# Turning x, k and q by transfers inside SBUF in a fused sparse-attention and maxout kernel

## The chip, the cores and the metric

One Trainium2 chip, one core of it. The metric is device time in microseconds (us) of one execution of the whole program. The kernel before took 181.66 us, the median of three runs (181.26 to 181.75). Engines are named as in the profile: PE is TensorE (PEld its weight loads), DVE is VectorE, ACT is ScalarE, POOL is GpSimd, SP is SyncE, which issues nearly all transfers; its queue appears as SPq.

## The reference

Inputs q, k, v have 4 batches, 8 heads, 768 positions of width 64. Each position attends to its neighbours less than 16 away and to 24 block summaries (k by maximum, v by mean, over 32 positions). The output goes through a maxout layer.

```
k_sum = k.reshape(B, H, nb, block, D).max(axis=3)        # block = 32, nb = 24
v_sum = v.reshape(B, H, nb, block, D).mean(axis=3)
scores_l = scale * q @ k.T, masked to |i - j| < 16
scores_s = scale * q @ k_sum.T + log(block)
a = softmax(concat(scores_l, scores_s)); attn = a @ concat(v, v_sum)
x = attn with the heads side by side                      # 3072 x 512
out = maximum(x @ w1, x @ w2) @ w_out                     # 512 -> 1024 -> 512
```

## The kernel before

**Stages.** The work of a batch is cut into four pairs of heads (`hp`) and three groups of 256 positions (`grp`). For each batch and pair, `load_kq` and `load_v` (L310, L317) bring k, q and v into SBUF as float32. `prep` (L404) casts k and q to bf16 (tile `kqb`), has PE turn them into a PSUM bank by `transpose` (op "turn", L422 to L431; k as three transposes of float32 pairs, q as six of bf16), and "place" copies them from the bank into `kx` and `qx` (DVE for k, ACT for q after batch 0). DVE then takes the block maxima (L449). `scores` (L470) multiplies on PE, ACT takes the exponential into `pb`, DVE masks it. `values` (L528) multiplies with `vx` on PE; DVE takes the reciprocal and scales into `xs` (L550, L552). After each second pair, PE turns the 128 x 512 block of x into a bank by four transposes (L562), and a copy (DVE after batch 0) brings it to `xt` (L567). `maxout` (L631) runs on `xt`: per batch and group four "hidden" steps (PE, then Relu on ACT) and "out" steps on PE, a copy from the bank and a store. Here maximum(h1, h2) is written as h1 + relu(h2 - h1), the first term through a product w1 x w_out that is made once.

**v.** `vx` holds v at even and at odd 64-position offsets. `cast_v` writes the even half; `spread_v` (L338) makes the odd half from it by three copies ("odd v", L352 to L363: 64 partitions by 3168 elements, 32 by 2640, 32 by 528) and spreads the sums of v. With engine "S" a copy is a transfer on SP (`move`, L386).

**Order.** The order of instructions is not written out by hand. `Plan` (L73) takes every operation with an engine, a cost, a priority and the buffers that it reads and writes, and lists them greedily, earliest possible first, by its own costs; each engine then runs its list strictly in order. Buffers come from rings of fixed size (`Ring`, L30); a DMA waits in SP's list for its source and its free target. Attention of batch b has priority 1000 b and on, `maxout` of batch b 1000 b + 1500 and on, so that maxout of one batch fills PE beside the attention of the next. The string `CFG` (L21) says which engine does what: `lod` is the engine of "odd v" of batches 1, 2, 3, `lk`, `lq` those of the casts.

```
op("PE", J * 0.056, turn, read=[src], write=[ps], prio=prio, label=f"turn {'kq'[n]}{tag}")      # L431
op("PE", 0.23, turn, read=[x], write=[xp], prio=prio, label=f"turn x{tag}")                     # L566
```

Of the kernel before, what the change touches and what calls it, by code (L numbers as in the profile page):

```python
# [13 lines left out]
BF16 = mybir.dt.bfloat16  # L14
# [7 lines left out]
    kc="DAPA", qc="AAAA", kp="DDDD", qp="AAAADAAA", tl="DDDD", od="DDDD", se="AAAA", sr="PPPP", vc="PPPP",  # L22
    wd="PDDD", w1b="PPAD", w1t="DADD", wo="AADD", xt="AADDDD", z="DAAA", kv=0.2, sp=0.7, ones=1, on="DDD", w=(30,
    31, 50, 51, 200, 201), wt=25, g0=(10, 30, 210), g1=(20, 30, 40), w1o=450, mx=1500, woc=600, wdp=30, lk="ADDP",
    lq="AAPA", lod="SSS", lse="DDD", lsr="DDS", lvc="DPPPDDAPPAPA", ltl="DDPD", ld=500,
)
ENG = {"D": "DVE", "A": "ACT", "P": "POOL"}

# [118 lines left out]
def kernel(  # L147
# [14 lines left out]
    nc = tc.nc  # L162
    B, H, S, D = 4, 8, 768, 64
# [10 lines left out]
    op = plan.op  # L174
# [4 lines left out]
    def tiles(name, n, shape, dt):  # L179
        return [const.tile(shape, dt, name=f"{name}{i}") for i in range(n)]  # L180
# [5 lines left out]
    def bank(buf, n=512, dt=F32):  # L186
        a = bank_tile[:, buf.slot]
        return (a if dt is F32 else a.bitcast(BF16))[:, 0:n]

    def spread(a, *dims):  # L190
        return bass.AP(a.tensor, a.offset, [a.ap[0], *dims])
# [5 lines left out]
    kqb = Ring(tiles("kqb", 4, [128, J * 2 * D], BF16))  # L197
    kxr = Ring(tiles("kx", 4, [128, KW], BF16))
    qxr = Ring(tiles("qx", 4, [128, 2, S], BF16))
    pbr = Ring(tiles("pb", 11, [128, 4, 192], BF16))  # L200
    vfr = Ring(tiles("vf", 4, [128, 2, NM, D], F32))
    vxr = Ring(tiles("vx", 2, [128, NT, H, VW], BF16))
    stg = Ring(tiles("sums", 1, [128, H, VW], BF16))
    ksr = Ring(tiles("ks", 2, [128, nb], BF16))
    xsr = Ring(tiles("xs", 4, [128, 2, 2, 2, D], BF16))
    xtr = Ring(tiles("xt", 6, [128, KC, GT], BF16))
    gr = Ring(tiles("g", 3, [128, FC, GT], BF16))
# [184 lines left out]
    def copy(engine, us, aps, label, port=True, **kw):  # L392
        engine = ENG[engine]
        us = us if isinstance(us, float) else us[engine[0]]
        def fn():
            o, i = aps()
            {"DVE": nc.vector.tensor_copy, "ACT": nc.scalar.copy,  # L397
             "POOL": nc.gpsimd.tensor_copy}[engine](out=o, in_=i)
        op(engine, us, fn, label=label, port=port, **kw)
# [4 lines left out]
    def prep(b, hp, prio, k_on, q_on, kp, qp, tail_on):  # L404
        kx[b, hp], qx[b, hp] = Buf(kxr), Buf(qxr)
        tag = f"{b}{hp}"
        pss = []
        for n, eng in enumerate((k_on, q_on)):
            f, src, ps = kqin[b, hp, n], Buf(kqb), Buf(banks, "kq")
            pss.append(ps)  # L410

            def cast(f=f, src=src, n=n):
                if n:
                    return (src.ap[:].rearrange("p (j h d) -> p h j d", h=2, d=D),
                            f.ap[:].rearrange("p h (j d) -> p h j d", d=D))
                return (src.ap[:].rearrange("p (i h d j) -> p h i j d", h=2, d=D, j=2),
                        f.ap[:].rearrange("p h (i j d) -> p h i j d", d=D, j=2))

            copy(eng, {"D": 0.6, "A": 0.85 if n else 1.06, "P": 0.8 if n else 1.05}, cast,
                 read=[f], write=[src], prio=prio, label=f"cast {'kq'[n]}{tag}")  # L420

            def turn(src=src, ps=ps, n=n):  # L422

                a, to, one = src.ap[:], bank(ps, S, BF16), identity
                if n == 0:
                    a, to, one = a.bitcast(F32), bank(ps), ident32
                for j in range(J if n else J // 2):
                    nc.tensor.transpose(out=to[:, 128 * j:128 * j + 128],  # L428
                                        in_=a[:, 128 * j:128 * j + 128], identity=one[:])

            op("PE", J * 0.056, turn, read=[src], write=[ps], prio=prio, label=f"turn {'kq'[n]}{tag}")  # L431

        kps, qps = pss

        def order(ps, *dims):
            return spread(bank(ps, S, BF16), *dims)

        def kt():

            return kx[b, hp].ap  # L440

        def pairs(at, step, n):
            return free(kt(), at, [256, NM], [step, 2], [1, n])

        kmain, ks, kwrap = Buf(Ring([None])), Buf(ksr), Buf(Ring([None]))
        copy(kp, {"D": 0.56, "A": 0.8}, lambda: (
            pairs(128, 192, 64), order(kps, [2, 128], [256, 3], [1, 2])),
           read=[kps], write=[kx[b, hp], kmain], prio=prio, port=False, label=f"place k{tag}")
        op("DVE", 0.95, lambda: nc.vector.tensor_reduce(  # L449
            out=ks.ap[:],  # L450
            in_=free(kt(), 128, [256, NM], [192, 2], [32, 2], [1, 32]),
            axis=AX.X, op=ALU.max),
           read=[kmain], write=[ks], prio=prio, label=f"max k{tag}")
        copy(tail_on, {"D": 0.18, "P": 0.15, "A": 0.25}, lambda: (
            kt()[:, 256 * NM + 128:256 * NM + 160], kt()[:, 128:160]),
           read=[kmain], write=[kx[b, hp], kwrap], prio=prio, label=f"wrap k{tag}")
        copy(tail_on, {"D": 0.27, "P": 0.45, "A": 0.5}, lambda: (
            pairs(192, 64, 32), pairs(320, 64, 32)),
           read=[kmain, kwrap], write=[kx[b, hp]], prio=prio, label=f"tails k{tag}")
        op("DVE", 0.24, port=True, fn=lambda: nc.vector.tensor_copy(  # L460
            out=pairs(224, 64, nb),
            in_=ks.ap[:].rearrange("p (a b n) -> p a b n", a=1, b=1).to_broadcast([128, NM, 2, nb])),
           read=[ks], write=[kx[b, hp]], prio=prio, label=f"sums k{tag}")
        for a in range(2):
            r = slice(64 * a, 64 * a + 64)
            copy(qp[a], {"D": 0.96, "A": 0.8}, lambda a=a, r=r: (
                qx[b, hp].ap[r, a, :], order(qps, [1, 128], [128, J])[r]),
               read=[qps], write=[qx[b, hp]], prio=prio, port=False, label=f"place q{tag}")

# [58 lines left out]
    def values(b, hp, grp, pb, prio, xt_on="D"):  # L528
        ps, tag = Buf(banks, "av"), f"{b}{hp}{grp}"

        def av():
            return bank(ps)[:, 0:4 * (D + 1)].rearrange("p (u a d) -> p u a d", u=2, a=2)

        def mm():
            for u in range(2):
                for a in range(2):
                    for par in range(2):
                        nc.tensor.matmul(out=av()[:, u, a, :],  # L538
                                         lhsT=pb.ap[:, 2 * u + a, 64 * par:64 * par + 128],
                                         rhs=vx[b].ap[:, 4 * grp + 2 * u + par, 2 * hp + a, 0:D + 1],  # L540
                                         start=(par == 0), stop=(par == 1))

        op("PE", 0.24, mm, read=[pb, ready[b, hp]], touch=[vx[b]], write=[ps], prio=prio, label=f"values {tag}")
        inv = Buf(invr)
        if hp % 2 == 0:
            xs[b, grp] = Buf(xsr)
        if hp == 0:
            xt[b, grp] = Buf(xtr)
        x, x_t = xs[b, grp], xt[b, grp]
        op("DVE", 0.18, lambda: nc.vector.reciprocal(out=inv.ap[:], in_=av()[:, :, :, D:D + 1]),  # L550
           read=[ps], write=[inv], prio=prio, label=f"inv {tag}")
        op("DVE", 0.42, lambda: nc.vector.tensor_tensor(  # L552
            out=x.ap[:, hp % 2], in0=av()[:, :, :, 0:D],
            in1=inv.ap[:].to_broadcast([128, 2, 2, D]), op=ALU.mult),
           read=[ps, inv], write=[x], prio=prio, label=f"x {tag}")
        if hp % 2 == 0:
            return
        xp = Buf(banks, "x")

        def turn():  # L560
            for n in range(4):
                nc.tensor.transpose(out=bank(xp, 512, BF16)[:, 128 * n:128 * n + 128],  # L562
                                    in_=x.ap[:, n // 2, n % 2].rearrange("p a d -> p (a d)"),
                                    identity=identity[:])

        op("PE", 0.23, turn, read=[x], write=[xp], prio=prio, label=f"turn x{tag}")  # L566
        copy(xt_on, {"D": 0.42, "A": 0.62}, lambda: (  # L567
            x_t.ap[:, hp - 1:hp + 1, :].rearrange("p h n -> p (h n)"), bank(xp, 512, BF16)), read=[xp], write=[x_t], prio=prio, port=False, label=f"xt {tag}")
# [115 lines left out]
    def attention(b, base):  # L684
        pbs = {}
        for hp in range(NP):
            p = base + 20 * hp
            prep(b, hp, p, CFG["lk"][hp], CFG["lq"][hp], "D", "AA", CFG["ltl"][hp])
            for grp in range(NG):
                pbs[hp, grp] = scores(b, hp, grp, p + 5 + grp, "DVE")  # L690
            for grp in range(NG):
                values(b, hp, grp, pbs[hp, grp], p + 10 + grp)

    def first_attention():
        pbs = {}
# [64 lines left out]
```

## Time and profile before

| what | value |
|---|---|
| median of three runs | 181.66 us (181.26 to 181.75) |
| span of the profiled execution, first to last instruction | 181.2 us |
| difference of the two, what lies around the span | 0.46 us |
| PE busy | 163.5 us, 1658 matmuls |
| ACT, DVE, POOL busy | 117.9, 106.6, 34.8 us |
| granted TensorE clock | 1.000 |
| moved by DMA | 33.96 MB, 187 GB/s over the span |

The profiled execution's own time is its span plus what lies around it; no separate time is given for it, so the span is set against the median. In the profile, "busy" of PE is modelled from pipelined matmuls: a single matmul's listed duration holds its latency, and what it takes from PE in a stream is read from the chain of waits, where pieces follow each other without overlap. The time of a transfer "to landing" runs from its issue to the event that tells that its data is there.

### The profile page before, as it was taken

The page shows a single profiled execution, that of the slowest core. Times are in us where ns is not written, and L with a number is a line of the kernel's source. Part 1 is how long each engine was busy: PE and PEld are TensorE (multiplying, and loading weights), DVE is VectorE, ACT ScalarE, POOL GpSimd, SP SyncE. Part 2 cuts the span into 40 slices and gives each one's busy share as a digit, 9 for nine tenths or more (in the row PEclk, how much of TensorE's full clock was granted, in tenths as well). Part 3 has the DMA queues.
Part 4 walks back from the last instruction along what each step waited for, and adds up shares of the span by engine and source line. Part 5 has one row for each costly group of instructions (what it writes and reads, how often), then busy time and mean ns, then how long its engine had stood idle before and what let it go on. Part 6 is the DMA issues. An engine that isn't in the chain of part 4 may idle for free.

```text
span 181.2 us, 4246 instructions
## 1 busy us (share of the span) xinstructions
PE 163.5 (90%) x1658; PEld 117.7 (65%) x1658; DVE 106.6 (59%) x314; ACT 117.9 (65%) x190; POOL 34.8 (19%) x61
## 2 busy tenths in 40 slices
PE   0496575999899999999999999999999999999992
PEld 0475475999355555688677685686786766575762
DVE  6699995977679775699796760388774400000000
ACT  8786965998739964289896642599975334352521
POOL 7776576010152000241070000001000000000000
PEclk9999999999999999999999999999999999999999
DMA  5999999999999999998996320340200113030203
GB/s 179 301 293 295 375 387 359 234 299 371 237 314 304 187 312 322 339 257 228 300 281 202 88 113 0 121 90 0 90 32 4 58 58 99 21 116 0 116 4 116
DMA packets 42820, 33.96 MB, mean 187 GB/s; under 512 B 26096, under 2 KB 36784, under 8 KB 42800
## 3 DMA queue, kind: packets, MB, share of 16 engines
q1 hardware_dynamic: 42656, 33.63, 64.4%
q8 instruction: 13, 0.21, 0.5%
q10 hardware_dynamic: 144, 0.07, 0.1%
q14 instruction: 7, 0.06, 0.1%
HBM read 25.17 MB, written 6.29 MB: 174 GB/s over the span
## 4 chain that ended last, share of the span: by engine, by line
PE 74%; DMA 13%; ACT 4%; SPq 4%; DVE 3%; issue 1%; ACTq 0%; DVEq 0%
PE banks L667 23%; PE banks L639 17%; PE banks L660 11%; DMA wf<-in_moe_w_dram 6%; DMA wf<-in_moe_w_out_dram 6%; PE banks L538 5%; PE banks L428 5%; PE banks L492 4%; PE banks L623 3%; PE banks L562 2%; PE banks L368 2%; SPq L580 2%; ACT qx L241 2%; DVE ks L449 1%; SPq L608 1%; DVE vx L397 1%
## 5 line engine op out<-in xcount | busy, mean ns | idle before, releaser
L667 PE MATMUL banks<-wo,g 128*128 128x512 bf16 (+2 forms) x208 | 46.8, 362 | 0.0
L639 PE MATMUL banks<-xt,wd 128*128 128x256 bf16 x384 | 46.3, 273 | 0.0
L639 PEld LDWEIGHTS <-wd 128*128 128x128 bf16 x384 | 36.7, 98 | 5.2
L644 ACT ACTIVATE g<-banks 128x512 bf16<-128x512 f32 x48 | 28.3, 597 | 9.9 <-PE banks L639 9.6
L397 ACT COPY o<-banks 128x512 f32<-128x512 f32 (+2 forms) x25 | 14.0, 564 | 29.8 <-PE banks L667 29.6
L504 ACT ACTIVATE pb<-banks 128x512 bf16<-128x512 f32 x48 | 27.3, 600 | 8.7 <-PE banks L492 7.1
L667 PEld LDWEIGHTS <-g 128*128 128x128 bf16 x208 | 18.2, 97 | 15.7
L397 ACT COPY qx<-banks 64x768 bf16<-64x768 bf16 x31 | 24.5, 791 | 1.8 <-PE banks L428 1.2
L660 PE MATMUL banks<-w1o,xt 128*128 128x512 bf16 (+2 forms) x104 | 24.2, 363 | 0.0
L397 ACT CAST kqb<-kqf 128x768 bf16<-128x768 f32 x18 | 16.1, 894 | 6.2 <-DMA kqf<-in_q_dram 3.5
L397 DVE COPY o<-banks 128x128 f32<-128x128 f32 x1 | 0.3, 292 | 32.2 <-PE banks L667 32.2
L552 DVE TENSOR_TENSOR xs<-banks,inv 128x256 bf16<-128x256 f32 x48 | 18.7, 413 | 0.2
L538 PEld LDWEIGHTS <-pb 128*128 128x128 bf16 x384 | 15.7, 97 | 4.7 <-ACT pb L504 1.1
L538 PE MATMUL banks<-vx,pb 128*128 128x65 bf16 x384 | 17.9, 193 | 0.9 <-ACT pb L504 0.9
L492 PE MATMUL banks<-qx,kx 128*128 128x128 bf16 (+2 forms) x208 | 16.8, 217 | 0.1
L492 PEld LDWEIGHTS <-kx 128*128 128x128 bf16 x208 | 14.1, 99 | 4.1 <-DVE kx L397 0.6
L397 DVE COPY xt<-banks 128x512 bf16<-128x512 bf16 x22 | 9.1, 423 | 10.5 <-PE banks L562 10.1
L449 DVE TENSOR_REDUCE ks<-kx 128x24 bf16<-128x768 bf16 x16 | 15.1, 941 | 0.2
L660 PEld LDWEIGHTS <-xt 128*128 128x128 bf16 x104 | 9.7, 98 | 8.0
L428 PE MATMUL banks<-identity,kqb 128*128 128x128 bf16 x96 | 8.3, 225 | 7.2 <-ACT kqb L397 7.2
L397 POOL CAST vx<-vf 128x768 bf16<-128x768 f32 x10 | 8.2, 824 | 32.3 <-DMA vf<-in_v_dram 32.1
L428 PEld LDWEIGHTS <-kqb 128*128 128x128 bf16 x96 | 6.5, 100 | 7.9 <-ACT kqb L397 7.4
(65 smaller groups left out, 179.5 us busy)
## 6 DMA issues: line engine op xcount, KB each, us to landing
kqf<-in_k_dram SPq DMA_DIRECT2D x16, 384.0 KB, 6.5
kqf<-in_q_dram SPq DMA_DIRECT2D x16, 384.0 KB, 5.6
vf<-in_v_dram SPq DMA_DIRECT2D x16, 384.0 KB, 6.5
out_dram<-o SPq DMA_DIRECT2D x19, 256.0 KB, 2.0
wf<-in_moe_w_dram SPq DMA_DIRECT2D x4, 1024.0 KB, 11.1
wf<-in_moe_w_out_dram SPq DMA_DIRECT2D x2, 1024.0 KB, 10.4
vx<-vx SPq DMA_DIRECT2D x3, 396.0 KB, 6.8
out_dram<-o SPq DMA_DIRECT2D x4, 224.0 KB, 3.3
```

The source lines that it names most:

```text
L397: {"DVE": nc.vector.tensor_copy, "ACT": nc.scalar.copy, "POOL": nc.gpsimd.tensor_copy}[engine](out=o, in_=i)
L428: nc.tensor.transpose(out=to[:, 128 * j:128 * j + 128], in_=a[:, 128 * j:128 * j + 128], identity=one[:])
L449: op("DVE", 0.95, lambda: nc.vector.tensor_reduce(out=ks.ap[:], in_=free(kt(), 128, [256, NM], [192, 2], [32, 2], [1, 32]), axis=AX.X, op= ...
L492: nc.tensor.matmul(out=o[:, :, n0:n1], lhsT=w, rhs=qx[b, hp].ap[:, :, c:c + n1 - n0], start=(mask_on != "PE"), stop=(mask_on != "PE" or (i ...
L504: op("ACT", 0.7, lambda: nc.scalar.activation(out=pv(), in_=bank(ps).rearrange("p (i w q) -> p i w q", w=2, q=64), func=ACT.Exp, scale=scale),
L538: nc.tensor.matmul(out=av()[:, u, a, :], lhsT=pb.ap[:, 2 * u + a, 64 * par:64 * par + 128], rhs=vx[b].ap[:, 4 * grp + 2 * u + par, 2 * hp ...
L552: op("DVE", 0.42, lambda: nc.vector.tensor_tensor(out=x.ap[:, hp % 2], in0=av()[:, :, :, 0:D], in1=inv.ap[:].to_broadcast([128, 2, 2, D]), ...
L623: nc.tensor.matmul(out=bank(ps), lhsT=w[:, at:at + 128], rhs=wo[f // 2].ap[:, f % 2, :], start=(f == 0), stop=(f == FC - 1))
L639: nc.tensor.matmul(out=bank(ps)[:, 256 * s:256 * s + 256], lhsT=wd[n].ap[:, c, 128 * s:128 * s + 128], rhs=x.ap[:, c, :], start=(c == 0), ...
L644: op("ACT", 0.6, lambda n=n, ps=ps: nc.scalar.activation(out=g.ap[:, 2 * n:2 * n + 2, :].rearrange("p f n -> p (f n)"), in_=bank(ps), func ...
L660: nc.tensor.matmul(out=bank(ps, c1 - c0), lhsT=x.ap[:, c, sl], rhs=w1o[c].ap[:, cols], start=(c == 0), stop=False)
L667: nc.tensor.matmul(out=bank(ps, c1 - c0), lhsT=g.ap[:, f, sl], rhs=wo[f // 2].ap[:, f % 2, cols], start=False, stop=(f == FC - 1))
```

## The change

x of batches 1 to 3, and k and q of batches 2 and 3, are turned by a transposing DMA from SBUF to SBUF on SP's queue (`dma_start_transpose`) in place of PE transposes into PSUM. For k and q the target is a new ring `kt` of two tiles, from which "place" copies in place of the bank; k is cast without the pairing that the float32 transposes needed. For x the target is `xt` itself, so the copy from the bank goes. "odd v" of batch 1 moves from SP to DVE, of batch 2 from SP to POOL. The ring `pb` goes from 11 to 9 tiles. The planner's costs of the new operations are in the diff.

```diff
-    lq="AAPA", lod="SSS", lse="DDD", lsr="DDS", lvc="DPPPDDAPPAPA", ltl="DDPD", ld=500,
+    lq="AAPA", lod="DPS", lse="DDD", lsr="DDS", lvc="DPPPDDAPPAPA", ltl="DDPD", ld=500,
+    turn="20 21 22 23 30 31 32 33", lx="SSS",
...
-    pbr = Ring(tiles("pb", 11, [128, 4, 192], BF16))
+    pbr = Ring(tiles("pb", 9, [128, 4, 192], BF16))
...
+    ktr = Ring(tiles("kt", 2, [128, J, 128], BF16))
...
+            by_dma = f"{b}{hp}" in CFG["turn"]
+            f, src, ps = kqin[b, hp, n], Buf(kqb), Buf(ktr) if by_dma else Buf(banks, "kq")
...
-                if n:
+                if n or by_dma:
...
-            op("PE", J * 0.056, turn, read=[src], write=[ps], prio=prio, label=f"turn {'kq'[n]}{tag}")
+            if by_dma:
+                op("SP", 1.0, lambda src=src, ps=ps: nc.sync.dma_start_transpose(out=ps.ap[:], in_=src.ap[:]),
+                   read=[src], write=[ps], prio=prio, label=f"turn {'kq'[n]}{tag}")
+            else:
+                op("PE", J * 0.056, turn, read=[src], write=[ps], prio=prio, label=f"turn {'kq'[n]}{tag}")
...
-            return spread(bank(ps, S, BF16), *dims)
+            return spread(ps.ap[:].rearrange("p j t -> p (j t)") if by_dma else bank(ps, S, BF16), *dims)
...
-        copy(kp, {"D": 0.56, "A": 0.8}, lambda: (
-            pairs(128, 192, 64), order(kps, [2, 128], [256, 3], [1, 2])),
+        copy(kp, {"D": 0.88, "A": 0.83, "P": 0.85} if by_dma else {"D": 0.56, "A": 0.8}, lambda: (
+            pairs(128, 192, 64), order(kps, [1, 128], [128, 6]) if by_dma else order(kps, [2, 128], [256, 3], [1, 2])),
...
+        if xt_on == "S":
+            op("SP", 0.7, lambda: nc.sync.dma_start_transpose(
+                out=x_t.ap[:, hp - 1:hp + 1, :].rearrange("p h (u n) -> p (h u) n", u=2),
+                in_=x.ap[:].rearrange("p h u a d -> p (h u a d)")),
+               read=[x], write=[x_t], prio=prio, label=f"xt {tag}")
+            return
...
-                values(b, hp, grp, pbs[hp, grp], p + 10 + grp)
+                values(b, hp, grp, pbs[hp, grp], p + 10 + grp, CFG["lx"][b - 1])
```

More of the change, by code (lines that the diff above doesn't have):

```diff
@@ L408, in prep @@
         for n, eng in enumerate((k_on, q_on)):
-            f, src, ps = kqin[b, hp, n], Buf(kqb), Buf(banks, "kq")
+            by_dma = f"{b}{hp}" in CFG["turn"]
+            f, src, ps = kqin[b, hp, n], Buf(kqb), Buf(ktr) if by_dma else Buf(banks, "kq")
             pss.append(ps)
             def cast(f=f, src=src, n=n):
-                if n:
+                if n or by_dma:
                     return (src.ap[:].rearrange("p (j h d) -> p h j d", h=2, d=D),
@@ L417, in cast @@
                         f.ap[:].rearrange("p h (i j d) -> p h i j d", d=D, j=2))
-            copy(eng, {"D": 0.6, "A": 0.85 if n else 1.06, "P": 0.8 if n else 1.05}, cast,
+            copy(eng, {"D": 0.6, "A": 0.85 if n or by_dma else 1.06, "P": 0.8 if n or by_dma else 1.05}, cast,
                  read=[f], write=[src], prio=prio, label=f"cast {'kq'[n]}{tag}")
@@ L465, in prep @@
             r = slice(64 * a, 64 * a + 64)
-            copy(qp[a], {"D": 0.96, "A": 0.8}, lambda a=a, r=r: (
+            copy(qp[a], {"D": 0.88, "A": 0.83, "P": 0.85} if by_dma else {"D": 0.96, "A": 0.8}, lambda a=a, r=r: (
                 qx[b, hp].ap[r, a, :], order(qps, [1, 128], [128, J])[r]),
```

## The prediction

> **What bounds the kernel now.** I read the page's busy row by slices first, then the table of stretches, then the chain of waits.
>
> ```profile
> PE   0496575999899999999999999999999999999992
> DMA  5999999999999999998996320340200113030203
> ```
>
> A slice is 4.5 us. PE is full from about 36 us to the end; the transfers fill the first 20 slices (to about 92 us) and are light after. The table of stretches puts numbers to it (us of the stretch, then busy us of PE, PEld, DVE, ACT, POOL, the clock, the DMA share, GB/s):
>
> ```profile
> 36.00:60.00 24.00, 23.42 (x192) 16.02 (x191) 18.12 (x39) 18.53 (x30) 5.46 (x8) 1.00 1.05 303
> 60.00:82.00 22.00, 22.00 (x241) 14.47 (x240) 15.89 (x49) 13.75 (x21) 3.41 (x4) 1.00 1.10 282
> 82.00:100.00 18.00, 18.00 (x208) 13.66 (x207) 14.87 (x44) 15.32 (x26) 3.57 (x7) 1.00 0.92 253
> 100.00:120.00 20.00, 20.00 (x191) 13.94 (x188) 10.05 (x32) 10.26 (x17) 0.00 (x0) 1.00 0.29 84
> 120.00:145.00 25.00, 25.00 (x302) 18.68 (x300) 17.09 (x59) 18.34 (x32) 0.72 (x2) 1.00 0.11 38
> ```
>
> PE has no idle time from 60 us on and the clock is full: in these stretches, where all removed work lies, PE sets the pace and its work taken away is time taken away, as long as nothing new makes it wait. Pieces of the chain of waits (start, us on the chain, what) give what an operation takes from PE in a full stream:
>
> ```profile
> 74.47 0.45 PE banks L562 x8
> ...
> 124.25 0.34 PE banks L428 x6
> ...
> 125.90 0.33 PE banks L428 x3
> ```
>
> Eight x transposes take 0.45 us, 56 ns each; the six of one q take 0.34, the three of one k 0.33. The 219 ns that the group table gives for one such matmul hold its latency, so I don't use them.
>
> **What is removed.** From PE: 18 turns of x (batches 1 to 3, three groups, two pairs of heads) of four transposes, 72 x 0.056 = 4.0 us; 8 turns of q (0.34) and 8 of k (0.33), 5.4 us. Together **9.4 us**, all between 74 and 145 us. From DVE 18 copies to `xt` (0.42 each), 7.6 us, no bound of itself. From SP six "odd v" transfers.
>
> **What is added, and what hides it.** DVE takes the three "odd v" of batch 1: its copy of 32 x 3168 elements took 978 ns, so 0.98 + 0.82 + 0.16 = 2.0 us, hidden since PE is the bound there and DVE has 6 us free in 22. POOL takes those of batch 2: 32 x 792 elements took 862 ns, 1.09 ns per element, so 3.4 + 2.9 + 0.6 = 6.9 us. In the order of the new program some 11 us of PE work stand between the last cast of that v and the first "values" of batch 2, and POOL had 3.4 to 3.6 us of work in stretches of 18 to 22 us: hidden, with about 2 us to spare; if late, PE waits for the excess. "place k" reads SBUF with a stride in place of packed pairs: between 0.55 us (now) and 0.93 (the one DVE copy of q, 934 ns), at most 8 x 0.38 = 3.0 us on DVE, which loses 7.6; nothing. "place q" stays near 0.79 on ACT. Casts of k lose their pairing: at most some tenths. `pb` at 9 tiles: three groups ahead in place of nearly four; the program now interleaves "values" of batch 1 earlier, and PE has its other work there; nothing.
>
> **The unknown: the transposing DMA itself.** No row shows one. A turn of k or q moves 192 KB, one of x 128 KB. The nearest rows are the plain SBUF to SBUF moves (the last number is us to landing):
>
> ```profile
> vx<-vx SPq DMA_DIRECT2D x3, 396.0 KB, 6.8
> ...
> vx<-vx SPq DMA_DIRECT2D x3, 165.0 KB, 4.8
> vx<-sums SPq DMA_DIRECT2D x2, 198.0 KB, 3.2
> ```
>
> The last one is the same size and ran at 117 us, beside nothing else: 3.0 to 3.5 us. While loads are in flight, a load takes 5.6 (q) or 6.5 us (k, v). The bounds are 2.0 us (the median of the stores) and 9.6 us (the slowest of the `vx` moves). I take **3.2 us in a quiet queue and 6.0 beside loads**, the row nearest in size and kind.
>
> What that costs: `kt` has two tiles, one for k and one for q of a pair, so the turn of the next q is issued only when both halves of the last are placed. The cycle is landing + 2 x 0.79 us of "place q" + 0.5 us of handover (estimate: a semaphore and half of a running 0.6 us instruction on ACT). PE hides it if the work that its list has between the first scores of one pair and of the next is longer. By the chain's pieces (scores 0.225, values 0.24, a hidden step 0.87, half an out 0.86, sums 1.29) the list of the new program has between successive pairs of batches 2 and 3: 6.6, 13.5, 6.4, then 7.2, 6.4, 6.0, 5.7 us. (The 6.0: 3 scores, 4 values, 3 out, 2 hidden.) Batch 2 is turned while the loads of batch 3 run: 6.0 + 2.1 = 8.1, so PE waits 1.5 + 0 + 1.7 = 3.2 us. Batch 3 has a quiet queue: 3.2 + 2.1 = 5.3, below every period, so 0. The x turns have a whole batch of time before `maxout` reads them and cost PE nothing, but they stand in SP's list between the turns of k and q, each waiting for DVE's "x". While ACT or DVE waits for a turn at its "place", the exp, Relu, masks and scalings behind it wait too, and PE for these; in batch 3 ACT has 20.7 us of work (12 exp, 8 halves of q, 8 Relu, 4 copies) beside 21.8 us of PE work, so I add 0.5.
>
> **Sum**: 181.2 - 9.4 + 3.2 + 0.5 = 175.5 us of span; with the 0.46 around it **176.0 us**. If every turn is hidden it is 171.8 + 0.46 = 172.3, the low end.
>
> The Trainium skill has two pages that disagree on the price. "Advanced Engine Details and Errata", X-Bar Transpose (TRN2), says that such transfers are as fast as plain ones, 350 to 400 GB/s; an estimate from it is 0.5 us of moving for 192 KB, and the sum stays as it is. "VectorE: DVE Perf Modes", The three transpose paths, gives 1309 ns by DMA for a 128 x 128 block against 390 on TensorE; no run here shows either yet (in this stream a bf16 block took PE 56 ns), and it speaks against the change.
>
> **Rivals.**
>
> 1. *The turns' cycle becomes the pace* (slower). If a turn lands E later than the plain move, all cycles grow by E, in batch 2 and 3. At E = 1.65 us (4.85 in the quiet queue) the waits are 6.5 + 2.8 = 9.3 us and the gain is used up; above, the kernel is slower. At E = 2.8: batch 2 4.3 + 0 + 4.5, batch 3 0.9 + 1.7 + 2.1 + 2.4, 15.9 in all: 181.2 - 9.4 + 15.9 + 0.46 = 188.2. SP can cause it alone: an issue held SP 0.38 to 0.48 us when the queue was free, and a pair has 2 turns and 1.5 x turns; beside 0.7 us of stores per pair, 5.3 us of a 6.0 us period are left, 1.5 us each. For it: ACT and DVE run in order, ACT is nearly full in batch 3, the list leaves 0.4 to 1.1 us per pair. Against: the plain move of that size.
>
> 2. *The turn goes block by block*, each with its own latency, so a turn of six blocks takes several times the plain move. With the slowest row, 9.6 us in the quiet queue (E = 6.4): batch 2 7.9 + 1.0 + 8.1, batch 3 4.5 + 5.3 + 5.7 + 6.0, 38.5 us: 210.8. Nothing in the trace speaks for it. By the VectorE page's 1309 ns, blocks in a row would be an estimated 7.9 us per turn, which is this rival.
>
> 3. *The gain is hidden or used up exactly*: DMA late by the added 5.5 MB, or ACT in batch 3 the bound: 181 to 182. Against it: the transfers are light from 92 us on.
>
> **How the numbers follow.** The forecast's case, 172.3 to 180.5, has 0.50. Within 0.3% of 181.66 (181.1 to 182.2, about what this kernel's measurement can tell from no change): 0.07. Rival 1, 182.3 to 195: 0.27. Rival 2, above 195: 0.16. The range for 8 in 10 runs from 172 to 193, leaving out the top of rival 1 and rival 2. Faster gets the forecast's 0.50, same 0.07, slower 0.43. Of the forecast's own case alone the range is 172 to 180.5.
>
> **What would show it.** Right: PE's busy time near 154 us and still 9 in every slice from 36 us to its end; the list of DMA issues shows the turns landing in 3 to 4 us after 100 us and 5 to 7 before; ACT and DVE wait little for `kt` at L397. Rival 1: waits of ACT and DVE for the transfer into `kt` of 1 to 3 us each, PE waiting for `kx` and `qx` in batches 2 and 3 between 80 and 145 us, SP's issues of the turns above 1.5 us. Rival 2: landings of 8 us and more, slices of PE at 5 or 6. Wrong altogether would be PE idle before 70 us, from the smaller ring `pb` or the moved "odd v", which I costed at nothing, or PE's waits at the first "values" of batch 2 behind POOL.

## The result and the profile after

The changed kernel took **192.37 us** (191.87 to 193.80, four runs) beside 181.70 for the kernel before: a ratio of 1.0605, 95% interval 1.0562 to 1.0648, 10.7 us slower. The prediction of 176.0 has the wrong sign; that the time still lies inside its wide range of 172 to 193 is luck, since that range reached up for rival 1, and most of the waits below are not rival 1's. The profiled execution took 191.87 us, its span is 190.2. So 1.7 us lie around the span, as in the other timed executions (181.21 us with a span of 179.5 in the kernel before), and not 0.46: the span of 181.2 on which the prediction stands belongs to an execution of the kernel before of some 182.9 us, 1.2 above the median.

The busy row by slices (now 4.75 us each) with the granted clock below it:

```profile
PE   0596688999999993649999699778998999999992
PEclk9999999999999999997999999979999999999999
DMA  5999999999999998998999799567436150220203
```

PE was full from 36 us on before; now it has holes from slice 15 (71 us) to slice 30 (147 us; the first slice is 0), and in two slices its clock falls. Slices 15 to 17 are the deepest. By stretches (columns as in the prediction):

```profile
60.00:70.00 10.00, 10.00 (x120) 6.08 (x118) 8.71 (x31) 7.02 (x11) 1.93 (x3) 1.00 1.24 269
70.00:80.00 10.00, 6.32 (x46) 2.99 (x43) 8.55 (x8) 5.73 (x7) 6.77 (x3) 1.00 0.86 225
80.00:90.00 10.00, 6.33 (x71) 5.04 (x72) 9.46 (x27) 6.53 (x11) 2.32 (x2) 0.83 0.91 159
...
120.00:130.00 10.00, 7.32 (x55) 5.15 (x53) 5.63 (x17) 7.48 (x9) 0.83 (x1) 0.83 0.72 152
...
140.00:150.00 10.00, 8.81 (x99) 6.23 (x97) 5.58 (x18) 9.42 (x15) 0.00 (x0) 1.00 0.41 88
```

From 70 to 80 us DVE is busy 8.55 of 10 us with *eight* instructions, beside POOL with three. From 140 to 150 it is ACT that is full. The start of each matmul against the usual distance to the one before it gives PE's waits: 18.8 us after 60 us, against 0.9 before. Ten waits above 0.3 us make 16.0 of them (3.11 at 75.8, 1.71 at 80.8, 2.85 at 84.2, 2.01 at 109.1, 2.85 at 124.9, 1.35 at 147.7 and four small ones); 2.6 are matmuls at half clock. With the 9.4 us taken off PE: 18.8 - 0.9 - 9.4 = 8.5 of the 9.0 us between the two profiled spans.

Who ends these waits (waits of all engines from 60 to 150 us; total, times, longest):

```profile
PE banks L545 <- DVE pb L520: 4.7, 3, 2.9
...
PE banks L499 <- ACT qx L399: 3.3, 3, 1.8
...
PE banks L499 <- DVE kx L399: 2.7, 1, 2.7
...
PE banks L652 <- DMA xt<-xs: 2.7, 1, 2.7
```

Four different causes, none the whole. The last one is a turn of x of batch 2: it was issued at 121.5 us, landed at 124.9, and PE waited for it until then. The turns themselves did as forecast in the quiet queue and better beside the loads. The issues of `kt` from 60 to 109.5 us (batch 2) and from 110 to 150 (batch 3), then those of `xt` (the last number is the median us to landing), and the issue's own time on SP (min/median/max ns):

```profile
kt<-kqb SPq DMA_TRANSPOSE x8, 3.8
...
kt<-kqb SPq DMA_TRANSPOSE x8, 2.9
...
xt<-xs SPq DMA_TRANSPOSE x15, 2.7
```

```profile
L435 SPq DMA_TRANSPOSE kt<-kqb x16: 1209/1238/2518, 66.5 to 140.6; - x16
```

Batch 3's turns landed in 2.7 to 3.5 us, beside the forecast's 3.2; batch 2's in 2.8 to 6.4, with a median of 3.8 beside the forecast's 6.0. But an issue holds SP for 1.24 us, with six blocks or four (`xt` 1.22). The prediction's 0.38 to 0.48 came from loads and stores; a plain move inside SBUF held SP 0.65 us at the median in the kernel before, and 0.59 at the least. What did not go as forecast is the copy that follows, "place q" (busy us, mean ns):

```profile
L399 ACT COPY qx<-kt 64x768 bf16<-64x768 bf16 x16 | 24.3, 1522 | 2.0 <-DMA kt<-kqb 1.8
...
L399 ACT COPY qx<-banks 64x768 bf16<-64x768 bf16 x15 | 11.9, 792 | 2.6 <-PE banks L431 2.2
```

The same copy, with the same step of 128 elements, takes ACT **1.52 us from SBUF and 0.79 from PSUM**. That is 16 x 0.73 = 11.7 us more on ACT. And POOL's copies of the odd v of batch 2 (three, 6.83 us), with what DVE did meanwhile (start, duration; two answers):

```profile
72.50 6.83 POOL L399 COPY vx<-vx 64x3168 bf16<-64x3168 bf16 x3 [5.12 <-ACT o L399]
```

```profile
72.73 3.04 DVE L520 TENSOR_TENSOR pb<-pb,mask 128x512 bf16<-128x512 bf16 x1
75.70 3.14 DVE L399 COPY kx<-kt 128x768 bf16<-128x768 bf16 x1
78.76 0.40 DVE L559 TENSOR_TENSOR xs<-banks,inv 128x256 bf16<-128x256 f32 x1
```

A mask that takes 0.40 us and a "place k" that takes 0.82 took 3.04 and 3.14. POOL's copies, one by one, took 2.99, 2.46 and 1.36: the mask ends 0.3 us after POOL's first, "place k" 0.82, its own length, after the second. DVE stood still during POOL's first two copies. Then POOL stood still: its third copy, of 528 elements, needs 0.50 us by the rate of its first (2.99 for 3168), and it ends 0.50 after "place k". The Trainium skill, "SBUF — State Buffer", Who interferes with whom, says that DVE and GpSimd share a pair of ports as an exclusive lock, held for a whole instruction: the trace agrees, 0.40 to 3.04 us.

### The profile page after: what moved, and what is told of

Same layout as the page of the kernel before. It is cut to its first block, busy times and chain, and to the rows that moved or that the text cites. A ratio compares the mean times of both kernels' runs of the same rounds, so it can differ in the third digit from the quotient of the medians.

```text
span 190.2 us, 3988 instructions
## 1 busy us (share of the span) xinstructions
PE 160.0 (84%) x1514; PEld 110.6 (58%) x1514; DVE 111.0 (58%) x297; ACT 128.4 (68%) x190; POOL 42.9 (23%) x64
## 4 chain that ended last, share of the span: by engine, by line
PE 48%; DMA 20%; DVE 12%; ACT 10%; issue 4%; SPq 3%; POOL 0%; ACTq 0%; DVEq 0%
PE banks L652 18%; PE banks L680 13%; PE banks L673 6%; DMA wf<-in_moe_w_dram 6%; DMA xt<-xs 6%; ACT qx L399 5%; DMA vf<-in_v_dram 3%; PE banks L499 3%; PE banks L545 3%; DVE kx L399 3%; DVE xs L559 2%; DMA kqf<-in_q_dram 2%; SPq L593 2%; ACT pb L511 2%; DMA vx<-sums 2%
## 5 line engine op out<-in xcount | busy, mean ns | idle before, releaser
L652 PE MATMUL banks<-xt,wd 128*128 128x256 bf16 x384 | 48.1, 282 | 2.7 <-DMA xt<-xs 2.7
L652 PEld LDWEIGHTS <-wd 128*128 128x128 bf16 x384 | 38.1, 101 | 9.4 <-issue 2.9
L680 PEld LDWEIGHTS <-g 128*128 128x128 bf16 x208 | 18.2, 97 | 15.9
L399 ACT COPY qx<-kt 64x768 bf16<-64x768 bf16 x16 | 24.3, 1522 | 2.0 <-DMA kt<-kqb 1.8
L545 PE MATMUL banks<-vx,pb 128*128 128x65 bf16 x384 | 18.7, 195 | 5.6 <-DVE pb L520 4.7
L545 PEld LDWEIGHTS <-pb 128*128 128x128 bf16 x384 | 16.3, 99 | 11.2 <-DVE pb L520 6.1
L499 PE MATMUL banks<-qx,kx 128*128 128x128 bf16 (+2 forms) x208 | 17.5, 222 | 6.0 <-ACT qx L399 3.3
L499 PEld LDWEIGHTS <-kx 128*128 128x128 bf16 x208 | 14.8, 101 | 10.8 <-issue 3.9
L520 DVE TENSOR_TENSOR pb<-pb,mask 128x512 bf16<-128x512 bf16 x24 | 12.9, 556 | 8.9 <-ACT pb L511 8.6
L557 DVE RECIPROCAL inv<-banks 128x4 f32<-128x4 f32 x48 | 7.8, 174 | 11.7 <-PE banks L545 11.1
L399 ACT COPY qx<-banks 64x768 bf16<-64x768 bf16 x15 | 11.9, 792 | 2.6 <-PE banks L431 2.2
## 6 DMA issues: line engine op xcount, KB each, us to landing
wf<-in_moe_w_dram SPq DMA_DIRECT2D x4, 1024.0 KB, 10.7
```

Source lines behind the costliest of these rows:

```text
L399: {"DVE": nc.vector.tensor_copy, "ACT": nc.scalar.copy, "POOL": nc.gpsimd.tensor_copy}[engine](out=o, in_=i)
L499: nc.tensor.matmul(out=o[:, :, n0:n1], lhsT=w, rhs=qx[b, hp].ap[:, :, c:c + n1 - n0], start=(mask_on != "PE"), stop=(mask_on != "PE" or (i ...
L520: eng.tensor_tensor(out=pv(), in0=pv(), in1=m, op=ALU.mult)
L545: nc.tensor.matmul(out=av()[:, u, a, :], lhsT=pb.ap[:, 2 * u + a, 64 * par:64 * par + 128], rhs=vx[b].ap[:, 4 * grp + 2 * u + par, 2 * hp ...
L652: nc.tensor.matmul(out=bank(ps)[:, 256 * s:256 * s + 256], lhsT=wd[n].ap[:, c, 128 * s:128 * s + 128], rhs=x.ap[:, c, :], start=(c == 0), ...
L680: nc.tensor.matmul(out=bank(ps, c1 - c0), lhsT=g.ap[:, f, sl], rhs=wo[f // 2].ap[:, f % 2, cols], start=False, stop=(f == FC - 1))
```

## The experiments

Theories, by the letters that some expectations use: **A**, POOL's copies stop DVE. **C**, place q at 1.52 us from SBUF makes the cycle of the two `kt` tiles longer and fills ACT. **D**, transfers issued while the loads run (before some 95 us) are late and make others late; in a quiet queue they are free. **E**, the planner's wrong costs give a bad list. Wherever a diff changes `CFG`, a ring or a cost, the planner makes a new list. The time of before in the four groups was 181.38 (e1 to e4), 181.48 (e5 to e8), 182.04 (e9 to e12) and 181.44 (e13 to e16).

**e1: odd v of batch 2 on DVE, list kept** (planned for POOL, issued on DVE).

```diff
+            if engines[0] == "P":
+                op("POOL", 0.06 + cols * 0.00095, lambda lo=lo, hi=hi, ms=ms, shift=shift: (
+                    lambda o, i: nc.vector.tensor_copy(out=o, in_=i))(*odd(lo, hi, ms, shift)),
+                   read=src, write=[*out, took], prio=prio, label=f"odd v{tag}{i}")
+                continue
```

> The changed kernel with its list of operations kept as it is, but the three copies of odd v of batch 2 issued on DVE at their place in place of POOL. Theory A (while POOL copies in SBUF, DVE's instructions with SBUF operands stand still: a mask of 0.40 us took 3.04, a place k of 0.82 took 3.14 beside POOL's copies of 2.99 and 2.46 us, and PE then waited 3.1 + 1.7 + 2.9 us at 75.8, 80.8 and 84.2 us): those DVE durations go back to 0.4 and 0.8, DVE works 2 us more, and the time falls by 4 to 7 us, to 185.5 to 188.5. Rival B (the turns' own latency through SP's queue sets the pace of batch 2): DVE's durations may change, the time does not, 191.5 to 193.

190.35 us (189.26 to 191.94), ratio 1.0473 (1.0393 to 1.0553). DVE's durations came back (place k at most 0.84) and the wait of 3.11 at 75.8 went, but the list was late a few us further on: PE waits 3.72 at 80.4 and 1.97 at 83.3. Only 2.0 us gained, with some 2 us of copies added to DVE: the stall is real, but something else is due right behind it.

**e2 and e3: place q reads rows and writes with a step** (e3 with e1 too). If the step of the read were what costs, the copy would fall back to 0.8.

```diff
-                qx[b, hp].ap[r, a, :], order(qps, [1, 128], [128, J])[r]),
+                (spread(qx[b, hp].ap[:, a, :], [1, J], [J, 128])[r], order(qps, [128, J], [1, 128])[r])
+                if by_dma else (qx[b, hp].ap[r, a, :], order(qps, [1, 128], [128, J])[r])),
```

> The changed kernel with the same list, but place q reads each of the six blocks of kt along its row (step of one element) and writes with a step of six elements, in place of reading with a step of 128 elements and writing along the row. Theory C (reading SBUF with that step makes ACT's place q 1.52 us in place of 0.79 from PSUM, 11.7 us more on ACT, and PE waits 0.4 + 2.0 + 1.4 us for qx): place q falls to 0.8 us and the time by 2 to 4 us, to 188.5 to 190.5. Rival B: 191.5 to 193, though place q is shorter. If place q stays at 1.5 us, the step is not the cause.

> Both edits, list unchanged. Theories A and C together: 11 us of the 18.8 us of PE waits after 60 us go, 181 to 184. Rival B: above 190.

The step in the write costs more still:

```profile
L399 ACT COPY qx<-kt x16: 2734/2761/2782, 76.0 to 155.7; 64x768 bf16<-64x768 bf16 x16
```

205.29 us, ratio 1.1246 (1.1142 to 1.1350); e3 204.51, ratio 1.1259 (1.1186 to 1.1331), where 181 to 184 was expected. As a repair it failed, and since it changes the step of the read and that of the write at once, what the read's step alone costs stays open; as a doubling of the disputed cost it serves: 16 x 1.24 = 19.9 us more on ACT gave 12.9 us more time, 0.65 us for one. "Place q" is on the path.

**e4: x alone** (batches 1 to 3; k and q by PE, odd v on SP, `pb` 11). **e5: x of batches 2 and 3 alone**, `lx="DSS"` in place of `"SSS"`.

```diff
-    lq="AAPA", lod="DPS", lse="DDD", lsr="DDS", lvc="DPPPDDAPPAPA", ltl="DDPD", ld=500,
-    turn="20 21 22 23 30 31 32 33", lx="SSS",
+    lq="AAPA", lod="SSS", lse="DDD", lsr="DDS", lvc="DPPPDDAPPAPA", ltl="DDPD", ld=500,
+    turn="", lx="SSS",
...
-    pbr = Ring(tiles("pb", 9, [128, 4, 192], BF16))
+    pbr = Ring(tiles("pb", 11, [128, 4, 192], BF16))
...
-    ktr = Ring(tiles("kt", 2, [128, J, 128], BF16))
+    ktr = None
```

> Only x of batches 1 to 3 is turned by transfers; k and q by PE, odd v of batches 1 and 2 by transfers on SP and 11 pb tiles, as before the change; the list is planned anew. If a turn of x costs PE nothing, 4.0 us of PE work go: 177.5 to 178.5, and PE never waits after 60 us. Rival B (turns in SP's order wait for DVE's x and hold up loads and stores, 1.2 us of SP each): 180 to 184, with PE waiting for xt or kqb.

> Only x of batches 2 and 3 is turned by transfers, all else as before the change, planned anew. Theory D (what costs is a turn that is issued while loads fill the queues, up to about 95 us: there it lands after 6 us and more, holds SP 1.2 to 2.5 us, and what stands behind it on SP and DVE is late; in the quiet queue it lands in 2.5 us and is free): 48 transposes of 0.056 us less on PE, 178.5 to 179.5, no PE waits after 60 us. Rival B (any turn costs through SP's order and the xs buffers that it holds): 181.5 to 185.

e4: 187.65 us, ratio 1.0310 (1.0247 to 1.0374), where 178 was expected. Its chain of waits (start, us, what):

```profile
71.39 6.01 DMA xt<-xs
...
78.94 0.29 SPq L566
...
79.33 4.66 DMA vx<-vx
...
84.08 0.17 DVE vx L399
84.25 4.90 DMA xt<-xs
```

Of the six turns of x of batch 1, issued beside the loads, these two land after 6.0 and 4.9 us (the other four after 3.1 to 4.5). DVE waits for the first with "x" and all that is behind it, and a plain move of v, which PE's "values" need, stands in SP's list behind a turn's issue: PE waits 4.18 us at 85.8, and its clock is at half from 84.0 to 90.8 us. e5, without batch 1: **179.53 us** (178.80 to 180.05), ratio 0.9868 (0.9801 to 0.9936), *faster than before*, no wait of PE above 0.3 us from 60 us on:

```profile
PE   0497599999999999999999999999999999999992
```

Its 12 turns of x (93 to 141 us) are hidden, and 1.95 of the 48 x 0.056 = 2.7 us are gained. The six turns of batch 1 make the 8.1 us between e4 and e5: for turns of x, D holds.

**e6: k and q of batch 3 alone.** **e7: k and q of batches 2 and 3, x by PE** (odd v of batch 1 on DVE, of 2 on SP).

```diff
-    turn="20 21 22 23 30 31 32 33", lx="SSS",
+    turn="30 31 32 33", lx="DDD",
```

(e6 with `lod="SSS"`; e7 with the turns kept, `lod="DSS"` and `lx="DDD"`.)

> Only k and q of batch 3 are turned by transfers (9 pb tiles, since kt needs the room), x by PE, odd v on SP. The queue is quiet there, so by theory D alone 2.7 us of PE work go: 179 to 179.5. Theory C (place q from kt takes ACT 1.52 us in place of 0.79, 5.8 us more for batch 3, where ACT has some 21 us of work beside 22 of PE): PE waits for qx 2 to 5 us and the time is 181 to 184.

> k and q of batches 2 and 3 by transfers, x by PE, odd v of batch 1 on DVE, of batch 2 on SP. 5.4 us of PE work go. Theories C and D: ACT has 11.7 us more to do and the turns of batch 2 fall among the loads: 183 to 189. If x turns alone were at fault (the run with x alone took 187.7): 177 to 180.

e6: 183.95 us (181.79 to 185.85, ten runs), ratio 1.0093 (1.0049 to 1.0136): 1.7 us slower by the ratio, 2.5 by the medians, where 4 x 0.67 = 2.7 are taken off PE. e7: 185.46, ratio 1.0193 (1.0113 to 1.0274): 3.5 to 4.0 slower where 5.4 are taken off. So the turns of k and q, with the smaller ring `pb` that both runs keep (and in e7 the odd v of batch 1 on DVE), cost some 4 to 5 us in batch 3 alone and 9 in batches 2 and 3. In e6 PE waits once, 3.0 us at 121.8: a turn of k was issued at 115.0 and landed at 119.3, and place k and the maxima came behind it. The execution profiled is the fastest of the ten, 181.79 us; what makes the others some 2 us longer no trace shows. In e7 ACT is busy 21.9 of 25 us from 120 to 145.

**e8: the kernel before with nothing but the odd v moved** (batch 1 to DVE, batch 2 to POOL).

```diff
-    lq="AAPA", lod="SSS", lse="DDD", lsr="DDS", lvc="DPPPDDAPPAPA", ltl="DDPD", ld=500,
+    lq="AAPA", lod="DPS", lse="DDD", lsr="DDS", lvc="DPPPDDAPPAPA", ltl="DDPD", ld=500,
```

> The kernel before with one edit, odd v of batch 1 on DVE and of batch 2 on POOL, planned anew; no transposing transfer. Theory A (POOL's copies make DVE stand still) says that masks or copies of DVE that fall beside the three POOL copies take 1.4 to 3 us and PE waits 0 to 4 us: 181.5 to 185. If the planner keeps them apart, 181 to 182, and theory A is tied to the lateness of the rest.

187.55 us, ratio 1.0301 (1.0230 to 1.0372): **this edit alone**, the odd v of both batches together, **costs 6.1 us.** POOL (first line) and DVE:

```profile
72.70 5.83 POOL L397 COPY vx<-vx 64x3168 bf16<-64x3168 bf16 x3 [3.88 <-DVE vx L397]
78.49 1.03 POOL L397 CAST kqb<-kqf 128x768 bf16<-128x768 f32 x1
```

```profile
76.24 0.69 DVE L397 CAST sums<-banks 128x512 bf16<-128x512 f32 x1 [3.69 <-PE banks L368]
76.84 0.55 DVE L397 COPY kx<-banks 128x768 bf16<-128x768 bf16 x1
77.43 0.95 DVE L449 TENSOR_REDUCE ks<-kx 128x24 bf16<-128x768 bf16 x1
78.30 2.48 DVE L513 TENSOR_TENSOR pb<-pb,mask 128x512 bf16<-128x512 bf16 x2
```

Two things to see. Beside POOL's copies DVE's reads of PSUM keep their times (0.69 and 0.55), and so does the maximum over `kx` (0.95); the masks, two sources in SBUF, do not: two of them take 2.48 us in place of 0.80, the first beside the end of POOL's copies, both beside its casts. And DVE stands idle for 3.69 us before: ACT had the scores ready by 73.9, but the list, in which the planner keeps DVE's SBUF work apart from POOL's, has the masks behind. Whether the list or the chip holds them, they come after POOL's copies, and PE's "values" wait (2.34, 0.53). Then PE's clock:

```profile
80.10:83.50 3.40, 2.76 (x38) 2.36 (x35) 3.19 (x9) 3.33 (x5) 1.53 (x3) 0.51 0.47 136
83.50:87.00 3.50, 3.50 (x21) 2.75 (x20) 2.70 (x6) 1.69 (x3) 0.00 (x0) 0.50 0.02 5
```

For 6.8 us after the wait PE runs at half clock (eight matmuls of a hidden step in 1.71 us in place of 0.87). The second stretch has no wait left in it and is still half as fast.

**e9: no POOL, no x of batch 1** (`lod="SSS"`, `lx="DSS"`, k and q as changed): A and the x turns of batch 1 are taken out, C and the k and q turns of batch 2 beside the loads are left.

> The changed kernel without its two parts that fall into the loading stage before 80 us: x of batch 1 turned by PE, odd v of all batches by transfers on SP; k and q of batches 2 and 3 and x of batches 2 and 3 by transfers as in the change; planned anew. 8.1 us of PE work go. Theory A and D (these two parts cost the most: odd v alone 6 us, x of batch 1 some 9 us) with C left in: 180 to 184. If k and q turns are the main loss: 186 or more.

201.73 us, ratio 1.1075 (1.1022 to 1.1128), far off the 180 to 184 expected; the rival, 186 or more if the turns of k and q are the main loss, is what came. Its chain shows the cycle of the two tiles:

```profile
116.15 3.40 DMA kt<-kqb
...
119.65 0.83 ACT kqb L399
120.48 1.55 ACT qx L399
...
122.04 1.49 ACT qx L399
...
123.55 4.49 DMA kt<-kqb
...
130.13 1.51 ACT qx L399
...
131.70 2.71 DMA kt<-kqb
```

A turn, the two places that free its tile, the next turn: some 8 us from turn to turn where the prediction had 5.3. PE waits four times for `qx`: 3.72, 7.74, 3.89 and 3.76 us, and its clock is at half for 20.5 us. This is not C alone: e7 has the same sixteen copies of "place q" and took 185.46 us. e9 adds the turns of x of batches 2 and 3 and the odd v of batch 1 to SP's list; from 102.6 to 116.1 us SP issued, one behind the other, three turns of x, two of k and q, a load, three moves of v and five stores, and the turn of 116.15 came after them. How the 16 us between e7 and e9 divide was not run.

**e10 to e12: can a better list mend it?** e11 is the changed kernel with true costs in the planner; e12 is e5 with the true time of an issue; e10 turns x of batches 2, 3 and k, q of batch 3 with true costs, half of the place q on DVE.

```diff
-                    busy[e] = now + self.ISSUE
+                    busy[e] = now + (1.24 if t.label[:2] in ("xt", "tu") else self.ISSUE)
...
-        copy(kp, {"D": 0.88, "A": 0.83, "P": 0.85} if by_dma else {"D": 0.56, "A": 0.8}, lambda: (
+        copy(kp, {"D": 0.82, "A": 1.52, "P": 0.85} if by_dma else {"D": 0.56, "A": 0.8}, lambda: (
...
-            copy(qp[a], {"D": 0.88, "A": 0.83, "P": 0.85} if by_dma else {"D": 0.96, "A": 0.8}, lambda a=a, r=r: (
+            copy(qp[a], {"D": 0.82, "A": 1.52, "P": 0.85} if by_dma else {"D": 0.96, "A": 0.8}, lambda a=a, r=r: (
```

> Only the turns in the quiet queue: x of batches 2 and 3, k and q of batch 3; odd v on SP. The first half of place q of batch 3 goes to DVE (0.82 us for such a copy there), and the planner is told 1.52 us for ACT's half, 0.82 for DVE's, 1.24 us of SP for a turn. 5.4 us less on PE: 176 to 177 if theory C is right that ACT's slow place q was what k and q of batch 3 cost; 179 or more if not.

> The changed kernel with nothing but the planner's costs put right (SP 1.24 us per turn, place q on ACT 1.52, place k on DVE 0.82); the work is the same, the order differs. Theory E (the work is not too much, the list was made for other costs, so engines wait in the wrong order): below 186. If the work itself is too much for its stage: 189 or more.

> The run with x of batches 2 and 3 alone (179.5 us), with the planner told 1.24 us of SP per turn. It had no PE wait above 0.25 us after 36 us, so nothing is left to win there: 179 to 180, unless the new order opens a wait.

e11: 193.59 us, ratio 1.0601 (1.0526 to 1.0675), nothing gained: for these costs E falls. e12: 179.38, ratio 0.9881 (0.9807 to 0.9955), as e5. e10: 182.64, ratio 1.0012 (0.9972 to 1.0053), where 176 to 177 was expected: on DVE place q takes 0.82, yet turning k and q of batch 3 as well still costs 2.4 (by the ratios) to 3.3 us (by the medians) against e12 of the same group. Its waits (1.06 at 114.6, 2.23 at 122.9) are for the turns and for moves of the sums that SP issues between them.

**e13 to e16: what divides the rest.** e13 is the changed kernel with `lod="DSS"`; e14 is e13 with `pb` of 7; e15 is e14 with four `kt` tiles; e16 is e6 with four `kt` tiles and `pb` of 7.

```diff
-    pbr = Ring(tiles("pb", 9, [128, 4, 192], BF16))
+    pbr = Ring(tiles("pb", 7, [128, 4, 192], BF16))
...
-    ktr = Ring(tiles("kt", 2, [128, J, 128], BF16))
+    ktr = Ring(tiles("kt", 4, [128, J, 128], BF16))
```

> The change without GpSimd's part: odd v of batch 2 by transfers on SP as before, all else as changed (the planner makes a new list). Theory A (the copies on POOL hold DVE, and this adds to the rest): no DVE instruction between 70 and 82 us above 1.6 us, TensorE's waits at 75 to 84 us (7.7 us in the changed kernel) mostly gone, 185 to 187.5 us. Rival (the parts overlap: the list is late there by the turns among the loads anyway, as in the run with odd v on DVE): 189 to 192 us, with waits of 5 us and more between 75 and 90 us by DMA or by kx and qx.

> The kernel of e13 with the ring pb of 7 tiles in place of 9, two tiles in kt: only the control for the next run, which needs the space. The size of pb costs nothing: within 1 us of e13. If the distance of scores and values is tight, 1 to 4 us more, with waits of values for pb.

> The kernel of e14 with four tiles in kt in place of two; the same work on every engine. Theory of the cycle (two tiles let one pair be turned at a time, landing 3 to 4.5 + two place q of 1.52): waits of scores for qx behind ACT behind 90 us fall from about 4 to 8 us to under 2, and 3 to 6 us less than e14. Rival (ACT's added 11.7 us of place q are the cost, wherever the tiles are): within 1 us of e14, the waits for ACT remain.

> The kernel of e6 (only k and q of batch 3 by transfer, 183.95 us) with four tiles in kt and pb of 7: the quiet queue alone. Theory of the cycle: the wait of 3.0 us at 121.8 us for qx goes, 178.5 to 181 us. Rival (ACT's place q fill it): 182 to 185, a wait for ACT remains.

| kernel | us | ratio to before |
|---|---|---|
| e13 | 196.20 (194.07 to 198.25) | 1.0773 (1.0692 to 1.0854) |
| e14 | 196.82 (196.33 to 199.01) | 1.0878 (1.0790 to 1.0967) |
| e15 | 190.88 (190.33 to 191.62) | 1.0521 (1.0470 to 1.0573) |
| e16 | 183.45 (182.56 to 184.01) | 1.0105 (1.0050 to 1.0160) |

e13 missed on both sides: without POOL the change is 3.8 us *slower*. The three moves of v of batch 2 now stand in SP's list (73.9 to 77.6 us), right ahead of a turn of k or q, and the list behind them is another one: in it PE waits 5.4 us, until 124.8, for a turn of x that SP issued at 121.4. How the 3.8 us divide between the two stays open. From 120 to 130 us ACT does 1.19 us of work in 10:

```profile
120.00:130.00 10.00, 5.24 (x32) 3.93 (x32) 4.73 (x12) 1.19 (x2) 0.72 (x2) 0.83 0.73 151
```

Four tiles, at the same work, take 5.9 us off (e15 against e14): ACT's work in that stretch is 6.69 us again and PE's wait there for x, 5.9 us in e14, is gone. My expectation that the waits for `qx` would go was wrong: behind 90 us they are 7.3 us in e15 against 3.3 in e14, each behind a place q of 1.5. With batch 3 alone (e16 against e6) four tiles give nothing that stands out of the spread, where 178.5 to 181 us was expected. So the two tiles cost where x and v share SP with the turns; the waits for ACT's longer copies are there in either case.

## Why the prediction was wrong, point by point

- **"No row shows one": the turn itself, 3.2 us quiet and 6.0 beside loads.** Right in the quiet queue (2.9 at the median in batch 3), too high beside the loads: batch 2's median was 3.8, and 6.0 is what its slowest took (5.8 and 6.4). Rival 2 had 7.9 or 9.6 for every turn; the longest of any run is 7.7 (e14, e15). An estimate by 1309 ns a block, which the Trainium skill has in "VectorE: DVE Perf Modes", The three transpose paths, would be 7.9 us for six blocks; the trace does not agree, 3.8 us beside the loads and 2.9 in the quiet queue for all six.
- **9.4 us off PE.** In size right as far as it was seen: 144 matmuls fewer, and e5 gives back 1.95 of its 2.7 us.
- **"'place q' stays near 0.79 on ACT".** Failed: 1.52. The row behind 0.79 was a copy from PSUM, and the source had changed. Put into the prediction's own sum: batch 2 has a cycle of 6.0 + 3.04 + 0.5 = 9.5 and waits 2.9 + 0 + 3.1; batch 3 has 6.7 and waits 0 + 0.3 + 0.7 + 1.0; 8.1 in place of 3.2, and 180.9 us. This term alone would use up the gain, though not more, and only with landings of 6.0 and 3.2 us. With those measured, 3.8 and 2.9, the waits are 0.7 + 0 + 0.9 and 0 + 0 + 0.4 + 0.7, or 2.9 with the roundings, and the sum is 175.7 again: the two errors cancel. PE's waits for `qx` in the changed kernel are 3.3 us, so the cycle as the prediction counted it is not where most of the loss lies. e2 shows that the copy is on the path all the same.
- **POOL "hidden, with about 2 us to spare".** This step failed most, and not by POOL's time: 6.83 us, as forecast (6.9). I asked who waits for the copy and not whom it stops. The sum had nothing for it; in the trace PE waits 4.7 us for masks and 2.7 for a copy of DVE into `kx`, the long ones from 72.9 to 84.2 us, beside POOL's copies and behind the work that they delayed. e8, with the odd v of batch 1 moved too: 6.1 us by itself, some 3 of them from the 6.8 us at half clock. What e1 gave back of it is 2.0 us, since other waits came in its place.
- **"The x turns ... cost PE nothing."** Right for batches 2 and 3 where PE turns k and q (e5), wrong for batch 1 among the loads: 8.1 us (e4 against e5). In the changed kernel one of batch 2 costs as well, 2.7 us at 124.9. I had given the turns of k and q a price there, and not the instructions that stand behind a late turn of x in SP's and DVE's lists.
- **The clock** has no term in the prediction; it assumed 1.00. Here it is half for two stretches of 3.4 us, 2.6 us lost.
- **odd v of batch 1 on DVE, `pb` at 9, the casts of k**: no wait of PE traced to them. `pb` at 7 cost 0.6 us by the medians (e14 against e13), and the intervals of the two ratios overlap. The step from 11 to 9 has no run of its own.
- **Rival 1** was nearest in size (188.2, or 188.7 with the 0.5 us that the main sum adds) and partly in kind: PE does wait for `qx`, but 3.3 us and not 15.9, and by the copies and not by the landing. SP's issue stayed below its 1.5 at the median, 1.24 us; single ones took 2.5.

The step that failed is thus the sum's rule of what PE waits for: the cycle of the two tiles and 0.5 us, with the moved odd v and the turns of x at nothing. Put there, 6.1 (e8) and 8.1 (e4 against e5) give 189.9 on top of 175.7, or 195.1 on top of 180.9, and the kernel took 192.4. That is no proof, for the costs do not simply add: e1, e9 and e13 say that a cause taken out opens the next, and the list moves. How the 18.8 us divide among A, C and D inside the changed kernel stays open; that each is real is shown by e8 for the moved odd v, by e2 for "place q", and by e4 against e5 for x of batch 1. The best kernel of the study is e5 (or e12), 1.3% below before: only the turns of x that fall into a quiet queue.

## What to carry to other kernels

A copy's price belongs to its source, destination and step together: where a change moves the source from PSUM to SBUF, find a row with that source, or bound it from both sides. For an engine with time to spare, ask not only whether it is done in time, but whom it stops while it works: in e8, copies that POOL had time for cost the kernel 6 us, since DVE's masks came behind them. And a transfer that replaces PE's work is free only where its queue and the lists behind it are free: sort the replaced operations by stage before pricing them as one.

## What the runs showed of the hardware

- ACT's copy of 64 x 768 bf16: 0.79 us from PSUM with a step of 128 elements, 1.52 from SBUF with the same step, 2.76 from SBUF in rows when written to SBUF with a step of 6. DVE copies the same from SBUF in 0.82.
- A transposing DMA from SBUF to SBUF holds SP for 1.24 us, of 128 or of 192 KB, beside 0.65 for a plain move inside SBUF and 0.4 to 0.5 for a load or store in a free queue; the longest took 2.52 in the changed kernel and 4.47 in e9 (at 98.1 us).
- Beside POOL's copies in SBUF, DVE's masks (two sources in SBUF) and its copy from SBUF waited for up to a whole POOL copy (0.40 to 3.04 us, 0.82 to 3.14); its reads of PSUM (0.55 and 0.69) and a maximum over one source in SBUF (0.95) did not. POOL's last copy in turn waited for DVE's.
- TensorE's granted clock goes to one half for one or more whole stretches of 3.4 us. The changed kernel's two:

```profile
84.90:88.30 3.40, 3.23 (x31) 2.24 (x29) 3.36 (x6) 3.40 (x6) 1.57 (x2) 0.50 0.66 154
...
125.90:129.30 3.40, 3.40 (x21) 2.52 (x19) 0.42 (x1) 2.96 (x4) 0.83 (x1) 0.50 0.71 154
```

A wait thus costs more than its length. What sets it off can be read by cutting each of the eighteen traces, from 30 us on, into stretches of 3.41 us at the edges that its clock shows, and adding up PE's idle time in each (by the modelled ends of the matmuls). Of the stretches at full clock, 22 had 2.09 us of idle or more, and each was followed by one at half; 741 had 1.93 or less, and none was. Half clock ended only behind stretches with 0.72 us of idle or less. So it is not a wait's length that counts but how much of it falls into one stretch: the wait of 3.11 at 75.8 lies across an edge at 74.7, with 1.8 us before and 1.2 behind it, and no fall came; those of 2.85 at 84.2 and 124.9 put 2.7 and 2.5 us into one. Before 30 us three falls came behind 1.7 to 2.0 us. The Trainium skill, "TensorE: Matmul & The Clock Gate", What's actually happening, has a window of 3413 ns and full speed only after a busy one; the trace agrees with the length, 3.4 us, and with the return. The Trainium skill puts the fall behind an idle window; here some 2.1 us of idle in one were enough.
